# Third stage of a fused attention and two-layer feed-forward kernel as seven block products for eight, slopes through DRAM, outputs summed in PSUM

## The chip, the cores and the metric

One NeuronCore of a Trainium2 chip runs the whole program. The metric is the device time of one execution in microseconds (us); a kernel is judged by the median of several runs. Engines are named as the profile names them: PE (matmuls) and PEld (its weight loads), DVE (vector engine), ACT (scalar engine), POOL and SP, which here mostly issue DMAs.

## The reference

Inputs are float64 in DRAM. Attention is over 4 batches, 12 heads, 448 positions and 64 columns; after it come two feed-forward layers over 1792 tokens.

```python
scores = scale * np.matmul(q, k.transpose(0, 1, 3, 2)) - np.log(S)
attn = 1.0 / (1.0 + np.exp(-scores))
x = np.matmul(attn, v)            # as 1792 x 768
h = np.maximum(np.maximum(x @ w1, x @ w2), x @ w3)      # 768 wide
y = h @ w_out                                            # 768 wide
a = y @ w_in                                             # 2048 wide
g = np.maximum(a, 0.0) + alpha * np.minimum(a, 0.0)      # "slopes"
out = g @ w_out2                                         # 768 wide
```

## The kernel before

Every operand of a matmul is kept as a high and a low part (two tiles of float32r, the low one the remainder), and a product of two operands is three matmuls: low by high, high by low, high by high. Weights come as pairs of 32-bit words in halves of 128 x 384 (`load_half`); `word_ops` (L180) makes float32 of a half with two ACT and three DVE operations (one of them a shift), and `split_ops` (L210) writes the two parts with a cast on ACT and a subtraction on DVE.

Activations are held transposed: 128 features on the partitions, tokens in the columns. The stages after attention are these.

- *First feed-forward product* (x by w1, w2, w3), in `ff1` (L614): 9 units of two feature blocks each, with the tokens in two halves `g`. One unit multiplies a 2 x 2 grid of blocks in seven products for eight (the Winograd form of Strassen's scheme): `unit_ops` (L243) forms seven factors from four weight halves, `form_ops` (L284) seven factors from four blocks of x, and `product` (L644) runs product `k` of unit `u` for half `g`: 9 matmuls of 448 columns into one of three banks X, V, W. At `k` = 0 ACT copies X into V, at 3 and 4 it copies X to the side; these copies stand between two products on the same bank. `evict` takes each finished block from PSUM and keeps the largest of three.
- *Second stage*, the c groups (`c_group`, L699): 24 groups of 18 matmuls of 448 columns. h is partly stored to and reloaded from DRAM through POOL's queue (`hd`, `reload`). y goes straight into the high and low tiles `yt`.
- *Third and fourth stage*, `ff2` (L781): 8 rounds `s` of two feature blocks of 128. `d_group` (L836) multiplies y by w_in, plainly: 18 matmuls for a block of 128 features by 512 tokens; the last 256 tokens are taken as one mixed group. `prelu` (L797) makes the slopes: two Relus on ACT, a join and a split. `e_tile` (L859) multiplies the round's two slope blocks by w_out2 for three tiles of 512 tokens: 6 matmuls into a bank, which DVE adds to an accumulator in SBUF (`acc`). `e_short` (L887) does the last 256 tokens with the slopes as the stationary operand, 384 columns. In the last round the sums are transposed and stored by `store` (L930).

The program is written out in one order by a planner of its own. Work for ACT and DVE is put on lists (`op`, L133), and `advance(cols)` (L138), called after each group of matmuls, takes from them what is ready, as far as a credit in columns goes; an operation costs its columns plus 150, and `STEP` is 1700. DVE's credit is at most what one call gives, ACT's two thirds of it. `need` and `need_ops` force what the next matmul wants. Each engine then runs its instructions in that order, waiting on semaphores.

SBUF slots come from pools of fixed size (`room`, L67; `wslot`, 23 weight slots, L72); a pool that is closed gives its room to the next.

Of the kernel before, what the change touches and what calls it, by code (L numbers as in the profile page):

```python
# [16 lines left out]
P = 128  # L17
# [4 lines left out]
def kernel(  # L22
# [44 lines left out]
    room = {"a": 28, "b": 48, "c": 24, "y": 4}  # L67
# [4 lines left out]
    def wslot(nm, dt=F32):  # L72
        return wpool.tile([P, HF], dt, tag="ws", name=nm, bufs=23)
# [10 lines left out]
    SK = 2  # L84
# [5 lines left out]
    for m in range(KDM):  # L90
        halves += [(w_o1, "col", m, h) for h in range(2)]
    for s in range(KF2 // SK):
        for w, kind in ((w_in, "col"), (w_o2, "row")):
            for f in range(SK):
                halves += [(w, kind, SK * s + f, h) for h in range(2)]
# [29 lines left out]
    class Op:  # L125
        def __init__(self, engine, cols, fn, deps, gate):
            self.engine, self.cols, self.fn, self.deps, self.gate = engine, cols + 150, fn, deps, gate
            self.step = None

# [3 lines left out]
    def op(engine, cols, fn, *deps, gate=None, soon=False):  # L133
        o = Op(engine, cols, fn, [d for d in deps if d is not None], gate)
        (urgent if soon else flow).append(o)
        return o

    def advance(cols, free=False):  # L138
# [3 lines left out]
        for todo in (urgent, flow):  # L142
            n = 0
            while n < len(todo):
                o = todo[n]
                if (
                    (free or o.engine == "Q" or credit[o.engine] > 0)
                    and all(d.step is not None and d.step < now[0] for d in o.deps)
                    and (o.gate is None or o.gate())
                ):  # L150
                    o.fn()
                    o.step = now[0]
                    if o.engine != "Q":
                        credit[o.engine] -= o.cols
# [6 lines left out]

    def need_ops(*ops):
        while any(o.step is None for o in ops):
            assert now[0] < 99999
            advance(0, free=True)

    def need(*dsts):
        for _ in range(99):
            if all(len(d) == 2 for d in dsts):
                return  # L170
            advance(0, free=True)
        raise AssertionError("an operand that nothing makes")
# [7 lines left out]
    def word_ops(z):  # L180
# [26 lines left out]
        o = op("A", 2 * HF, first, gate=lambda: z in since and now[0] > since[z] + 2)  # L207
        return op("D", 3 * HF, whole, o)

    def split_ops(dst, nm, src, pool, w, *deps, seen=lambda x: x, put=lambda x: x, **kw):  # L210

        def hi():
            dst[0] = wslot(f"{nm}h", F32R) if pool == "w" else slot(f"{nm}h", pool, w, F32R)
            nc.scalar.copy(put(dst[0]), seen(src()))  # L214

        def lo():
            dst[1] = wslot(f"{nm}l", F32R) if pool == "w" else slot(f"{nm}l", pool, w, F32R)
            nc.vector.tensor_sub(put(dst[1]), seen(src()), put(dst[0]).bitcast(F32))

        return op("D", w, lo, op("A", w, hi, *deps, **kw), soon=kw.get("soon", False))  # L220

    def conv_ops(z, gate=None):
        if z >= NZ:
            return
        wsp[z] = {}
        o = word_ops(z)
        if halves[z][1] == "col":
            split_ops(wsp[z], f"w{z}", lambda: word[z], "w", HF, o, gate=gate)
        else:
            split_ops(  # L230
                wsp[z], f"w{z}", lambda: word[z], "w", HF, o, gate=gate,
                seen=lambda x: x.rearrange("p (g m j) -> p m g j", g=4, m=HK),
                put=lambda x: x.rearrange("p (m g j) -> p m g j", g=4, m=HK),
            )

# [7 lines left out]
    def unit_ops(u):  # L243

        z = 4 * u
        f = wf[u] = [{} for _ in range(7)]
        t = {}

# [13 lines left out]
        def cut(k, src, *deps):  # L262
            gate = (lambda: (u - 1, k, 1) in made) if u else None
            return split_ops(f[k], f"f{u}_{k}", src, "w", HF, *deps, gate=gate)
# [5 lines left out]
        w2, w3 = word_ops(z + 2), word_ops(z + 3)  # L270
# [8 lines left out]

    wf = {}  # L280
    xf = {(g, c, r): {} for g in range(2) for c in range(7) for r in range(HK)}
    x32, fdone = {}, {}

    def form_ops(i):  # L284

        g, r, n = i // 12, i % 12 // 4, i % 4
        B11, B21, B12, B22 = (4 * (i // 4) + z for z in range(4))
        T1 = ("T", B12)

        def cut(c, src, *deps):  # L290
            pool = "b" if g == 0 or (r == 0 and c in (0, 1, 2)) else "a" if r < HK - 1 else "c"
            fdone[B11, c] = split_ops(
                xf[g, c, r], f"x{g}_{c}_{r}", lambda: x32[src], pool, TW, *deps,
                gate=lambda: pool in pools,
            )

        def t1():
            x32[T1] = slot(f"t1_{i}")
# [11 lines left out]
        if n == 0:  # L310
            cut(0, B11)
        elif n == 1:
            cut(1, B21)
        elif n == 2:
            fdone[B11, "t1"] = op("D", TW, t1)
            cut(2, T1, fdone[B11, "t1"])
        else:
            o3 = op("D", TW, t3, fdone[B11, "t1"])
            o2 = op("D", TW, t2, fdone[B11, 2])
            cut(3, T1, o2)  # L320
            cut(4, B12, o3)
            cut(5, B21, op("D", TW, t4, o2, fdone[B11, 1]))
            cut(6, B22)

    def attention(apool, ps_s, ps_v):
# [180 lines left out]
        def to_x(i):  # L506
            x32[i] = slot(f"x{i}")
            nc.scalar.copy(x32[i], pv.pop(i)[:, :S])
            form_ops(i)
# [28 lines left out]
        for i in range(0, n, 2):  # L538
            for z in range(2):
# [7 lines left out]
                if i + z == 18:  # L547
                    unit_ops(0)
# [33 lines left out]
    yt, ht, hd = {}, {}, {}  # L582
# [31 lines left out]
    def ff1(ps_m, dpool, swap):  # L614
        NU = 3 * HK
        cur, banks, side = {}, {}, {}

        def evict(u, g, i, t, src, other=None):

            j = u % 3  # L620
# [14 lines left out]
            if j == 2:  # L635
# [4 lines left out]
                else:  # L640
                    ht[m, t] = {}
                    split_ops(ht[m, t], f"h{m}_{t}", lambda: c, "b", TW, soon=True)

        def product(u, k, g):  # L644
            left = wf[u][k]
            need(left, *(xf[g, k, r] for r in range(HK)))
# [4 lines left out]
                        tuple(xf[g, k, r][x] for x in range(2)),  # L651
# [5 lines left out]
            nm = f"b{u}_{g}"  # L657
# [27 lines left out]
        def reload(m, t, gate, later):  # L685
            ht[m, t] = {}
            pool = "b" if t < 2 else "y"
            s = {}

            def load():  # L690
# [344 lines left out]
```

## Time and profile before

| | us |
|---|---|
| median of 3 runs | 929.83 (927.98 to 934.37) |
| profiled execution, its own time | 934.59 |
| its span, first to last instruction | 932.8 |
| PE busy | 922.8 |
| DVE busy | 613.3 |
| ACT busy | 446.4 |
| POOL busy | 71.7 |

All numbers from a trace are of the one profiled execution. A span is shorter than that execution's time by what lies before its first and after its last instruction. Matmuls overlap, so a matmul's own duration is longer than its share of a stretch: prices are read as a stretch divided by its count. A row of a stretch gives the stretch, its length, the busy times of PE, PEld, DVE, ACT and POOL with their counts, PEclk (the granted share of PE's full clock), the DMA engines' busy share and GB/s.

### The profile page before, as it was taken

The numbers are of one execution on the slowest core, as the hardware profiler recorded it, in microseconds if no ns is written. First come the engines' busy times: TensorE is split into PE (matmuls) and PEld (weight loads), VectorE is DVE, ScalarE is ACT, GpSimd is POOL, SyncE is SP. The second block draws the span as 40 slices with busy tenths as digits, with TensorE's granted clock in tenths as the row PEclk, the third lists the DMA queues.
The fourth block names the chain that finished last, engine by engine and source line by source line (L and its number), as shares of the span: only waits on it lengthen the run. The fifth ranks groups of instructions, "written<-read, shape, count | busy, mean of one in ns | idle before, by whom it ended". The sixth has DMA issues, their size and how long they took to land.

```text
span 932.8 us, 12606 instructions
## 1 busy us (share of the span) xinstructions
PE 922.8 (99%) x4712; PEld 758.7 (81%) x4712; DVE 613.3 (66%) x1187; ACT 446.4 (48%) x878; POOL 71.7 (8%) x115
## 2 busy tenths in 40 slices
PE   9999999999999999999999999999999999999997
PEld 5555548999999999989988888888888888888886
DVE  5888886677566568653454367676666866568675
ACT  5888886434433445442366551634506345063410
POOL 4433310001001001100000000000000000000001
PEclk9999999999999999999999999999999999999999
DMA  7888451333113224311221211212112121122126
GB/s 156 149 174 145 98 114 37 100 87 114 49 45 135 68 68 148 113 44 58 68 70 51 63 39 52 67 51 68 35 51 69 51 68 34 51 69 52 33 66 172
DMA packets 148573, 74.24 MB, mean 80 GB/s; under 512 B 94128, under 2 KB 144656, under 8 KB 148512
## 3 DMA queue, kind: packets, MB, share of 16 engines
q1 hardware_dynamic: 140704, 57.60, 24.5%
q0 software_dynamic: 5664, 14.98, 4.8%
q10 hardware_dynamic: 2144, 0.85, 0.3%
q8 instruction: 37, 0.61, 0.3%
q14 instruction: 24, 0.20, 0.1%
HBM read 64.23 MB, written 9.18 MB: 79 GB/s over the span
## 4 chain that ended last, share of the span: by engine, by line
PE 96%; ACT 2%; DMA 1%; DVE 1%; issue 0%; SPq 0%; ACTq 0%; DVEq 0%
PE d L604 25%; PE e L604 21%; PE c L604 9%; PE b_0X L604 7%; PE b_1X L604 7%; PE pav L485 6%; PE sc L464 6%; PE b_1W L604 4%; PE b_0W L604 4%; PE e_short L906 4%; PE b_1V L604 2%; PE b_0V L604 2%; ACT a L475 1%; DMA kr<-in_k_dram 0%; DMA kn<-in_k_dram 0%; DVE accs L917 0%
## 5 line engine op out<-in xcount | busy, mean ns | idle before, releaser
L820 DVE SCALAR_TENSOR_TENSOR r<-n,nalpha,r 128x512 f32<-128x512 f32 (+1 forms) x64 | 43.1, 683 | 100.5 <-ACT n L817 99.4
L879 DVE TENSOR_TENSOR acc<-e,acc 128x512 f32<-128x512 f32 x126 | 86.7, 688 | 23.9 <-PE e L604 21.7
L816 ACT ACTIVATE r<-d 128x512 f32<-128x512 f32 (+1 forms) x50 | 29.5, 590 | 146.9 <-PE d L604 146.9
L475 ACT ACTIVATE a<-sc,bias_s 128x896 f32<-128x896 f32 x84 | 82.1, 1014 | 13.4 <-PE sc L464 13.2
L485 PE MATMUL pav<-a,vt 128*64 128x448 f32 (+1 forms) x384 | 70.3, 551 | 0.0
L188 ACT ACTIVATE wt<-wr 128x384 f32<-128x384 f32 x112 | 61.8, 551 | 11.5 <-DMA wr<-in_moe_w_dram 5.9
L203 DVE CUSTOM_DVE_ANT_0 wt<-wr,wt 128x768 uint16<-128x768 uint16 x112 | 62.5, 558 | 3.9
L195 DVE SCALAR_TENSOR_TENSOR wr<-wr 128x384 uint32<-128x384 uint32 x112 | 62.1, 554 | 1.1
L191 ACT ACTIVATE wr<-wr 128x384 uint32<-128x384 uint32 x112 | 61.9, 553 | 0.0
L485 PEld LDWEIGHTS pav<-a,vt 128*64 128x64 f32 (+1 forms) x384 | 21.0, 135 | 38.5 <-issue 36.5
L194 DVE TENSOR_SCALAR wt<-wt 128x384 uint32<-128x384 uint32 x112 | 39.8, 355 | 14.2 <-ACT wt L188 14.2
L934 POOL DMA_DIRECT2D out_dram<-o x6 | 3.9, 663 | 525.4 <-DVE o L854 525.4
L725 DVE TENSOR_TENSOR yl<-c,yh 128x448 fp32r<-128x448 f32 (+5 forms) x36 | 14.2, 421 | 41.6 <-ACT yh L721 29.9
L386 POOL DMA_DIRECT2D vt<-in_v_dram x46 | 35.4, 771 | 63.9 <-PE pav L485 63.9
L464 PE MATMUL sc<-qh,kh 64*128 64x448 f32 x192 | 38.2, 394 | 2.1 <-ACT f_2h L214 1.3
L721 ACT CAST yh<-c 128x448 fp32r<-128x448 f32 (+5 forms) x36 | 12.2, 375 | 50.2 <-PE c L604 50.2
L464 PE MATMUL sc<-ql,kh 64*128 64x448 f32 x192 | 35.4, 365 | 0.0
L464 PE MATMUL sc<-qh,kl 64*128 64x448 f32 x192 | 35.1, 361 | 0.0
L464 PEld LDWEIGHTS sc<-qh,kh 64*128 64x128 f32 x192 | 18.0, 184 | 20.6 <-ACT a L475 6.1
L817 ACT ACTIVATE n<-d 128x512 f32<-128x512 f32 (+1 forms) x50 | 29.2, 585 | 0.0
L673 ACT COPY u<-b_0X 128x448 f32<-128x448 f32 x18 | 9.6, 533 | 39.7 <-PE b_0X L604 39.7
L239 DVE TENSOR_TENSOR u<-b_0W,u 128x448 f32<-128x448 f32 x12 | 7.5, 624 | 31.5 <-ACT u L673 26.3
(1834 smaller groups left out, 2668.5 us busy)
## 6 DMA issues: line engine op xcount, KB each, us to landing
wr<-in_moe_w_out_dram SPq DMA_DIRECT2D x44, 384.0 KB, 3.6
wr<-in_moe_w_dram SPq DMA_DIRECT2D x36, 384.0 KB, 3.6
wr<-in_moe_w_in_dram SPq DMA_DIRECT2D x32, 384.0 KB, 3.6
kr<-in_k_dram SPq DMA_DIRECT2D x92, 56.0 KB, 2.9
qr<-in_q_dram SPq DMA_DIRECT2D x92, 56.0 KB, 2.6
vt<-in_v_dram POOLq DMA_DIRECT2D x46, 96.0 KB, 3.2
hd<-mx POOLq DMA_DIRECT2D x16, 224.0 KB, 2.2
hr<-hd POOLq DMA_DIRECT2D x16, 224.0 KB, 3.7
```

Of the source, the lines that this page charges most:

```text
L188: nc.scalar.activation(st["T"].bitcast(F32), st["r"][:, :, 1].bitcast(F32), AF.Abs, scale=2.0**-112)
L191: nc.scalar.activation(st["r"][:, :, 0], st["r"][:, :, 0], AF.Copy, scale=2.0**-29)
L194: nc.vector.tensor_scalar(st["T"], st["T"], 3, None, ALU.logical_shift_left)
L195: nc.vector.scalar_tensor_tensor(out=st["r"][:, :, 0], in0=st["r"][:, :, 1], scalar=0x80000000, in1=st["r"][:, :, 0], op0=ALU.bitwise_and, ...
L203: nc.vector.tensor_tensor(out=st["T"], in0=st["r"][:, :, 0], in1=st["T"], op=ALU.add)
L464: nc.tensor.matmul(sc[:, j, :S], kx[r, c0 : c0 + P], qx[r], start=(start and z == 0), stop=(stop and z == 2),)
L475: nc.scalar.activation(a, sc[:, :, :S], AF.Sigmoid, bias=bias_s, scale=scale)
L485: nc.tensor.matmul(pv[i][j * D : (j + 1) * D, :S], vts[i][r, j, c, :], a[r, j, :], start=start, stop=stop,)
L604: nc.tensor.matmul(ps[:, : rh.shape[-1]], lt, rh, start=(start and z == 0), stop=(stop and z == len(mms) - 1), skip_group_check=True,)
L820: nc.vector.scalar_tensor_tensor(out=r_, in0=n_, scalar=nalpha[:, m : m + 1], in1=r_, op0=ALU.mult, op1=ALU.add,)
L879: nc.vector.tensor_tensor(out=acc[m, t], in0=ps, in1=acc[m, t], op=ALU.add)
L906: nc.tensor.matmul(ps, lt, rh, start=(f == 0 and i == 0), stop=(f == SK - 1 and i == 2))
```

## The change

The third stage is done like the first. y blocks are first copied to float32, then `form_ops` makes seven factors of each four blocks (`yf`); `unit_ops` makes those of w_in; 8 further units `u` = 9 to 16 run through `product`. `evict` hands their blocks to a new `prelu`, which stores the slopes as float32 to DRAM (`gd`). The c groups go in another order (four blocks that belong together follow each other), some of the conversions into other pools. Two larger pools, "a" and "c", give way to "e" and "l" at the end of the stage.

The fourth stage (`ff3`) then runs by token tiles: 48 steps, one for a tile `t` of 512 tokens and a block `f` of slopes, each 6 x 3 matmuls. Six banks, one for each output block, are summed over six blocks `f` and later over ten for the first two tiles, over all sixteen for the third. Slopes are reloaded through POOL's queue into three raw buffers and split again. All of w_out2 is kept in SBUF; it is converted 8 halves before the stage and 24 in it. The last 256 tokens come at the end, 48 matmuls into one bank for each of four blocks. `need_ops` now forces only what its operations depend on; before, it took everything that was ready.

```diff
-    room = {"a": 28, "b": 48, "c": 24, "y": 4}
+    room = {"a": 76, "c": 24, "e": 16, "l": 32}
...
+    blocks = [m for r in range(HK) for m in (r, r + HK)]
...
     def need_ops(*ops):
+        chain = [o for o in ops if o.step is None]
+        for o in chain:
+            chain += [d for d in o.deps if d.step is None and d not in chain]
         while any(o.step is None for o in ops):
...
-            advance(0, free=True)
+                for o in [o for o in todo if o in chain]:
+                    if ready(o) and (
+                        o.gate is None or o.gate()
+                    ):
+                        emit(o)
+                        todo.remove(o)
+            if len(urgent) + len(flow) == n:
+                advance(0, free=True)
...
+        def prelu(u, g, i, t, src, add=None):
+            f, b = 2 * (u - ND0) + i, 2 * g + t
+            s, o = {}, None
+            if add is not None:
+                o = op("D", TW, lambda: tensor_op(add, src, add, ALU.add), soon=True)
+            def parts():
+                x = src if add is None else add
+                s["r"], s["n"] = slot(f"r{f}_{b}"), slot(f"n{f}_{b}")
+                nc.scalar.activation(s["r"], x, AF.Relu)
+                nc.scalar.activation(s["n"], x, AF.Relu, scale=-1.0)
+            def join():
+                nc.vector.scalar_tensor_tensor(
+                    out=s["r"], in0=s["n"], scalar=nalpha[:, f : f + 1], in1=s["r"],
+                    op0=ALU.mult, op1=ALU.add,
+                )
+            def store():
+                if f not in gd:
+                    gd[f] = dpool.tile([P, B * S], F32, tag=f"g{f}", name=f"gd{f}")
+                nc.gpsimd.dma_start(out=gd[f][:, b * S : (b + 1) * S], in_=s["r"])
+            o = op("A", 2 * TW, parts, o, soon=True)
+            stored.append(op("Q", 0, store, op("D", TW, join, o, soon=True)))
...
         def evict(u, g, i, t, src, other=None):
+            if u >= ND0:
+                return prelu(u, g, i, t, src, other)
...
+        def y_home(g, c, r):
+            return "c" if g and (r == HK - 1 or (r == 1 and c >= 3)) else "a"
+        def y_gate(g, r):
+            if g == 0:
+                return lambda pool: r < HK - 1 or ("c", KDM - 1, 1) in made
+            if r == 0:
+                return lambda pool: ("c", KDM - 1, 1) in made
+            return lambda pool: ("c", *((HK, 3) if pool == "a" else (KDM - 1, 3))) in made
...
-            for t, (c0, w) in enumerate(spans):
-                c, e = max(c0, b * S), min(c0 + w, b * S + S)
-                if c < e:
-                    y_ops(t, m, slice(c - c0, e - c0), ps[:, c - b * S : e - b * S], e - c)
+            def out():
+                x32["y", m, b] = slot(f"y{m}_{b}", "c")
+                nc.scalar.copy(x32["y", m, b], ps[:, :TW])
+            o = op("A", TW, out, soon=True)
+            blk = [("y", r + HK * n, 2 * g + c) for c in range(2) for n in range(2)]
+            form_ops(f"y{g}{r}", 2 * t + i, blk, (g, r), yf, y_home, y_gate(g, r), o)
...
+        units(ND0, ND1 - 1, begin, (
+            (0, 1), (0, 0), (1, 1), (2, 1), (1, 0), (3, 1), (2, 0), (4, 1), (3, 0), (5, 1), (4, 0),
+            (6, 1),
+        ), lambda x: x == (5, 1) and started.append(ff3(ps_m, turn_left, E0)))
+        run = started[0]
+        swap()
+        for k in range(5, 7):
+            step(ND1 - 1, k, 0)
+        need_last = list(stored)
+        run(need_last)
...
+    def ff3(ps_m, turn_left, E0):
+        F1 = 6
+        passes = [(t, *x) for x in ((0, F1), (F1, KF2)) for t in range(2)] + [(2, 0, KF2)]
+        steps = [(t, f, f == f0, f == f1 - 1) for t, f0, f1 in passes for f in range(f0, f1)]
...
+        for n, (t, f, _, _) in enumerate(steps):
+            s, load = load_g(t, f, functools.partial(raw_g, n, t, f))
+            o = op("Q", 0, load, gops[n - 3] if n > 2 else None, gate=lambda n=n: n < 2 or "e" in pools, lag=4 if n > 2 else 1)
+            gops.append(
+                cut_g(
+                    s,
+                    lambda x, t=t, f=f: pools["e"].tile(
+                        [P, EW], F32R, tag=f"g{x}", name=f"g{x}{t}_{f}", bufs=3
+                    ),
+                    lambda s=s: s["t"],
+                    EW,
+                    o,
+                    lambda n=n: "e" in pools and (n < 3 or ("e", n - 3) in made),
+                    True,
+                )
+            )
+        for n in range(2 * E0, 2 * KF2):
+            pool = "e" if n < 4 * E0 else "l"
+            conv_ops(NE + n, pool, gate=lambda pool=pool: pool in pools)
...
+        def run(stored):
+            ps, done = {}, []
+            for n, (t, f, start, stop) in enumerate(steps):
+                if n == 2:
+                    need_ops(*stored)
+                    turn_left()
+                z = NE + 2 * f
+                need(wsp[z], wsp[z + 1])
+                need_ops(gops[n])
+                for m in range(KDM):
+                    if start:
+                        ps[m] = bank(ps_m, f"e{t}_{f}_{m}")
+                    a, b = three(weight(z, m), tuple(gt[t, f][x] for x in range(2)))
+                    group(ps[m], a + b, start=start, stop=stop)
+                    if stop:
+                        leave(t, m, ps[m], f < F1 or t == 2, f == KF2 - 1, done)
+                    if m == KDM - 1:
+                        made.add(("e", n))
+                    advance(2 * STEP // 5)
...
+            for n in range(HW // P):
+                for h in range(2):
+                    p = bank(ps_m, f"es_{n}{h}")[:, :HF]
+                    for f in range(KF2):
+                        need_ops(gops[len(steps) + f])
...
+                        advance(STEP // 3)
+                    x = pools["l"].tile([P, HF], F32, tag="acc", name=f"os{n}{h}", bufs=2 * KDM)
+                    nc.scalar.copy(x, p)
```

`leave` copies a finished bank to an accumulator with ACT, or adds it with DVE in a tile's second pass, and then has DVE transpose it; a tile's four stores go out on SP's queue.

## Rows read from the trace of the kernel before

**Rows 1.** The page's first lines: the span, and busy us, share and count of PE.

```profile
span 932.8 us, 12606 instructions
PE 922.8 (99%) x4712; PEld 758.7 (81%) x4712; DVE 613.3 (66%) x1187; ACT 446.4 (48%) x878; POOL 71.7 (8%) x115
```

**Rows 2.** Waits of PE from 142 us on: in total us, times, longest.

```profile
PE e_short L906 <- ACT g L826: 1.1, 1, 1.1
PE c L604 <- DVE h_3l L218: 0.2, 1, 0.2
```

**Rows 3.** The chain in order of time: start us, us, what, instructions.

```profile
174.44 1.86 PE b_1V L604 x9
...
380.90 14.89 PE c L604 x72
...
465.91 28.74 PE d L604 x132
494.64 24.49 PE e L604 x108
519.13 4.31 PE e_short L906 x24
...
868.52 24.48 PE d L604 x108
...
917.48 4.32 PE d L604 x36
923.46 2.80 PE e_short L906 x14
926.28 2.17 DVE accs L917 x4
```

**Rows 4.** Engines by stretch (us): first stage's products, c stage; us, busy us, PEclk.

```profile
142.60:375.30 232.70, 232.70 (x1128) 211.30 (x1127) 155.04 (x307) 105.37 (x224) 13.02 (x24) 1.00 0.27 85
375.30:466.00 90.70, 90.45 (x444) 82.81 (x443) 46.24 (x106) 34.43 (x88) 4.27 (x8) 1.00 0.24 71
```

**Rows 5.** Groups of ACT, 142.6 to 375.3 us: count, busy us, mean ns, idle.

```profile
L188 ACT ACTIVATE wt<-wr 128x384 f32<-128x384 f32 x36 | 19.8, 550 | 5.9 <-DMA wr<-in_moe_w_dram 5.9
L673 ACT COPY u<-b_0X 128x448 f32<-128x448 f32 x18 | 9.6, 533 | 39.7 <-PE b_0X L604 39.7
L214 ACT CAST f_2h<-wu 128x384 fp32r<-128x384 f32 x8 | 4.1, 517 | 0.0
```

**Rows 6.** Groups of ACT, 466 to 581 us.

```profile
L816 ACT ACTIVATE r<-d 128x512 f32<-128x512 f32 x12 | 7.2, 599 | 19.0 <-PE d L604 19.0
L826 ACT CAST g_2h<-r 128x512 fp32r<-128x512 f32 x4 | 2.5, 622 | 1.6 <-DVE r L820 1.6
L913 ACT COPY accs<-e_short 128x384 f32<-128x384 f32 x4 | 1.9, 480 | 2.3 <-PE e_short L906 2.3
```

**Rows 7.** Groups of DVE, 142.6 to 375.3 us.

```profile
L203 DVE CUSTOM_DVE_ANT_0 wt<-wr,wt 128x768 uint16<-128x768 uint16 x36 | 20.1, 558 | 1.2
L194 DVE TENSOR_SCALAR wt<-wt 128x384 uint32<-128x384 uint32 x36 | 12.8, 355 | 9.2 <-ACT wt L188 9.2
L239 DVE TENSOR_TENSOR u<-b_0W,u 128x448 f32<-128x448 f32 x12 | 7.5, 624 | 31.5 <-ACT u L673 26.3 <-PE b_0W L604 5.2
L218 DVE TENSOR_TENSOR f_1l<-wt,f_1h 128x384 fp32r<-128x384 f32 x8 | 4.4, 554 | 1.6 <-ACT f_1h L214 1.6
```

**Rows 8.** Groups of DVE, 466 to 581 us.

```profile
L820 DVE SCALAR_TENSOR_TENSOR r<-n,nalpha,r 128x512 f32<-128x512 f32 x12 | 9.0, 751 | 30.8 <-ACT n L817 30.5
L829 DVE TENSOR_TENSOR g_2l<-r,g_2h 128x512 fp32r<-128x512 f32 x4 | 2.8, 689 | 1.4 <-ACT g_2h L826 1.4
```

**Rows 9.** DMA issues: queue, count, KB each, median us to landing.

```profile
wr<-in_moe_w_out_dram SPq DMA_DIRECT2D x44, 384.0 KB, 3.6
...
hd<-mx POOLq DMA_DIRECT2D x16, 224.0 KB, 2.2
hr<-hd POOLq DMA_DIRECT2D x16, 224.0 KB, 3.7
```

More of the change, by code (lines that the diff above doesn't have):

```diff
@@ L89 @@
     NB = len(halves)
-    for m in range(KDM):
+    blocks = [m for r in range(HK) for m in (r, r + HK)]
+    for m in blocks:
         halves += [(w_o1, "col", m, h) for h in range(2)]
[L92 to L95, printed above, removed]
+    ND = len(halves)
+    for fp in range(KF2 // 2):
+        halves += [(w_in, "col", 2 * fp + z // 2, z % 2) for z in range(4)]
+    NE = len(halves)
+    for f in range(KF2):
+        halves += [(w_o2, "row", f, h) for h in range(2)]
     NZ = len(halves)
@@ L147, in advance @@
                     (free or o.engine == "Q" or credit[o.engine] > 0)
-                    and all(d.step is not None and d.step < now[0] for d in o.deps)
+                    and ready(o)
                     and (o.gate is None or o.gate())
                 ):
[L151 to L154, printed above, removed]
+                    emit(o)
                     todo.pop(n)
@@ L741, in ff1, with units @@
-        order = [(0, k, 0) for k in (0, 2, 1, 3)]
-        order += [(0, 0, 1), (0, 4, 0), (0, 2, 1), (0, 5, 0), (0, 1, 1), (0, 6, 0), (0, 3, 1)]
-        order += [(1, 0, 0), (0, 4, 1), (1, 1, 0), (0, 5, 1), (1, 0, 1), (0, 6, 1), (1, 1, 1)]
-        order += [(u, k, g) for u in range(1, L) for k in range(7) for g in range(2) if (u, k) > (1, 1)]
-        order += [(L, k, g) for k, g in (
+        def units(first, last, begin, end, before=None):
+            u, v = first, first + 1
+            o = [(u, k, 0) for k in (0, 2, 1, 3)]
+            o += [(u, 0, 1), (u, 4, 0), (u, 2, 1), (u, 5, 0), (u, 1, 1), (u, 6, 0), (u, 3, 1)]
+            o += [(v, 0, 0), (u, 4, 1), (v, 1, 0), (u, 5, 1), (v, 0, 1), (u, 6, 1), (v, 1, 1)]
+            o += [(n, k, g) for n in range(v, last) for k in range(7) for g in range(2) if (n, k) > (v, 1)]
+            o += [(last, k, g) for k, g in end]
+            for x in o:
+                if before and x[0] == last:
+                    before(x[1:])
+                step(*x)
@@ new lines, in leave, with room @@
+        def leave(t, m, ps, first, final, done):
+            def room():
+                if t not in ot:
+                    ot[t] = pools["l"].tile(
+                        [P, EW // 32, KDM, 32], F32, tag="ot", name=f"ot{t}", bufs=2
+                    )
+                turn(t, m)
+            if first:
+                acc[t, m] = pools["l"].tile([P, EW], F32, tag="acc", name=f"acc{t}_{m}", bufs=2 * KDM)
+                nc.scalar.copy(acc[t, m], ps)
+                spend("A", EW)
+            else:
+                tensor_op(acc[t, m], ps, acc[t, m], ALU.add)
+                spend("D", EW)
+            if final:
+                done.append(op("D", EW, room))
+                if m == KDM - 1:
+                    op("Q", 0, lambda: put(t), *done)
```

552 lines of the change are left out of this document (252 added, 300 removed).

## The prediction

> **What bounds the kernel now.** I read the page's busy shares first. TensorE (PE) is busy 922.8 us of a span of 932.8 [rows 1], so what the change does to PE's own instructions counts in full, and another engine counts only where PE comes to wait for it. The waits of PE come next: from 142 us to the end they add up to 1.3 us, in two waits [rows 2]. There are no stalls to win; a gain has to come from fewer or shorter matmuls, and a loss from new waits. The chain of work in order of time then gives the price of each kind of matmul, as stretch by count: a block product of the first feed-forward stage is 9 matmuls of 448 columns in 1.86 us, 206.7 ns each; the c groups run at the same pace (72 in 14.89 us); e (512 columns) takes 24.49 us for 108, 226.8 ns each; e_short (384 columns) 4.31 us for 24, 179.6 ns each; d, which mixes 512 and 256 columns, 28.7 us for 132 [rows 3]. An e group puts six matmuls into a bank, a d group eighteen, and both take 24.5 us for 108 matmuls of 512 columns, so leaving a bank for the next costs nothing. The granted clock is 1.00, the 2.4 GHz level, throughout [rows 4].
>
> The last look is at the two engines that feed PE, by stage. In the block products of the first stage VectorE (DVE) is busy 155 of 232.7 us and ScalarE (ACT) 105; in the c stage 46 and 34 of 90.7 [rows 4]. This is the room that the change will use up.
>
> **What is removed from PE.** The d stage is, in the chain, seven rounds of 28.7 us, then 24.48 and 4.32 us: 229.8 us [rows 3]. In its place stand 8 units of 7 products for 2 halves of the tokens, 9 matmuls each: 8 x 14 x 9 = 1008 matmuls of 448 columns. The same form runs before in the first stage, so its price is a row, not a guess: 1008 x 206.7 ns = 208.3 us. The saving is 21.5 us, less than an eighth (28.7), because the products also go from 512 columns to 448 and a narrower matmul costs more for each column: 226.8 ns for 512, 206.7 for 448.
>
> The Trainium skill, page "TensorE: Matmul & The Clock Gate", section "Back-to-back issue gap", gives the gap of a single warm matmul as columns / 2.4 plus 2.5 ns, so 189.2 ns for 448. The rows do not agree: 206.7 for 448 columns. By the page the old stage would cost 217.7 us and the new one 190.7, a saving of 27.0 us for 21.5.
>
> The e stage keeps 3 tiles x 16 x 6 x 3 = 864 matmuls of 512 columns, and the short block 2 x 2 x 16 x 3 = 192 of 384: 864 x 226.8 ns = 195.9 us and 192 x 179.6 ns = 34.5 us. Summed into fewer, longer accumulations they cost PE the same. From the first d to the last e_short before is 465.91 to 926.26, 460.35 us, with the one wait of 1.1 us in it [rows 2, 3]; after it is 208.3 + 195.9 + 34.5 = 438.7 us. That is 21.6 us less. The c stage keeps its 24 groups of 18 matmuls in another order, at no price.
>
> **The tail.** After the last matmul four additions by DVE (2.17 us) stand on the chain, and then the store [rows 3]. After the change the last short block is copied once by ACT from PSUM, 0.48 us by the same shape's copy [rows 6], then stored. That saves 1.7 us. The transposes and stores of the third tile lie under the 34.5 us of short blocks, and each tile has two more DMAs on SP's queue (its four stores no longer alternate with POOL), with nothing behind them there but two stores of short blocks. Removed without effect: the additions of every round (126 on DVE), which nothing waited for.
>
> So far 21.6 + 1.7 = 23.3 us.
>
> **What is added, and what hides it.** All prices of ACT and DVE below are from [rows 5 to 8]. *c stage.* Each output block is copied by ACT (0.53), and six sets of four blocks are combined (24 DVE operations of 0.62) and cut into high and low parts (42 casts of about 0.57 between the 384 and the 512 forms, 42 subtractions of 0.62): 36.6 us on ACT and 41 on DVE. With the weights (8 halves at 1.6 and 2.0 us), the cuts of h (8 pairs) and the first unit's factors the stage asks for some 62 us of ACT and 74 of DVE in 91 us of PE: it fits. Eleven cuts of the last two blocks wait for the last c group, since their slots hold h until then. They take about 6.3 us of ACT; the first product that needs one of them comes after four other products, 7.4 us, and the next ones at intervals of about two products. The blocks are also done in that order, so I cost this at nothing; with the cover gone it would be 6 us.
>
> *d stage.* For one unit, 26.0 us of PE: ACT has 4 weight halves (two operations of 0.55 each), 7 casts (0.52), 6 PSUM copies (0.53) and 16 Relu parts (0.55, between the 448 copy and the 512 Relu): 20.0 us, 77%. DVE has 4 x (0.56 + 0.56 + 0.35), 4 sums and 7 subtractions of 0.55, 4 additions of 0.62 and 8 joins of about 0.68 (0.75 for 512): 19.9 us, 76%. In the last unit 8 halves of w_out stand for the factors: 25 of 26 us on ACT and 24 on DVE. That is the tightest stretch ahead of the end, but w_out is needed a pair of halves for every step of 4.1 us later, not at once. The 64 stores of slopes go through POOL's queue, which holds nothing else then; stores of this size land in 2.2 us [rows 9].
>
> *The trip through DRAM.* Each of 48 steps of e loads 512 columns, in three raw buffers. A buffer's round is landing 3.7 us [rows 9], cast 0.62, subtraction 0.69: 5.0 us in three steps, 12.2 us. The first steps read slopes of the first unit, written 180 us earlier. So it is hidden with 7 us to spare. The Trainium skill, page "SBUF — State Buffer", section "Who interferes with whom", speaks against this move: descriptors of DMAs that GpSimd issues are held up while VectorE runs an operation in a two-port mode. The shift on the weights, 0.35 us and one for each half [rows 7], would be such an operation, and even one in front of every load would leave the 7 us nearly whole. The trace before has stores and reloads of h in that queue, landing in 2.2 and 3.7 us while DVE was two thirds busy, and shows no hold-up of its own.
>
> *Opening of e.* Here 24 halves of w_out are still to be converted. The kernel's planner gives DVE 680 columns for each 0.68 us group; a half costs 1836 of them and a slope tile 662, so 1.86 halves a step are put in. In time that is 1.86 x 2.02 + 0.69 = 4.45 us of DVE in a step of 4.08 us. DVE falls 0.37 us a step behind, for 13 steps: 4.8 us. Slope tiles are written out about 11 groups, 7.5 us, ahead of their use; 4.8 + 0.69 fits into that with 2 us left. The weights' landing of 3.6 us [rows 9] with three buffers (3.6 + 1.1 + 1.5 = 6.2 us for three halves, wanted every 6.6) is as close. If one of these covers is gone, what is late is the next slope tile, and PE with it.
>
> **Sum.** For handovers (c to d, d to e, e to the short blocks) and the opening of e I add a loss. The lower bound is 0, as in every handover of before; the upper is 9 us, all of DVE's 4.8 us twice over, once for itself and once for the loads. The chain of Relus, join and cut ahead of the last short block takes 1.66 us, from the end of the last d (917.48 + 4.32) to 923.46 [rows 3]. Three places with such a chain half covered make 2.5 us; I take this, near to the lower end, since the rows show hardly a wait. The profiled execution took 934.59 us, of which 932.8 are its span; it becomes 934.59 - 23.3 + 2.5 = 913.8 us. It lay 4.8 us above the median of the three runs, 929.83. Against the median: 929.83 - 20.8 = **909.0 us**.
>
> **Rivals.** *A: the opening of e is not covered.* DVE at over 100% of PE's pace and ACT near it speak for it; the lead of 7.5 us against. Loss 6 to 13 us: 913 to 920 us. *B: the copies between products are late (the other side).* In every unit 6 times, 48 times in all, PE waits for an ACT copy of a bank (the start of V, the two side sums) that must be done within one product, 1.86 us. The copy takes 0.53, so 1.3 us are left. With a pair of Relus (1.1) and a pair of weight operations (1.1) put ahead of it that only then begin, it comes 2.2 + 0.53 - 1.86 = 0.87 us late; 48 x 0.87 = 42 us, and the time is 948 us. It decides from 0.49 us a copy, where the gain is gone. Against it: in the first stage the same copies, with ACT at 45%, cost PE nothing [rows 2, 4], and the planner limits what stands ahead of a copy. With a third of that lateness (14 us) the time is 921. *C: the slopes land late*, held up in POOL's queue while DVE is near full. A buffer's round would have to grow from 5 to over 12 us; the landings of before speak against it. At 13 us a round it is 0.27 us a step, 13 us in all: 920 us. *D: a narrower matmul costs no more for a column*: the stage falls by a full eighth, 28.7 us for 21.5, and the time is 902 us; against it stand the 206.7 ns of the products before [rows 3]. The Trainium skill's page on TensorE, section named above, would give 903.5. That the change leaves PE's work as it was can't be: the count of matmuls is in the loops.
>
> **Chances.** Forecast (0 to 6 us lost, 906 to 913) 0.62; A 0.17; B 0.11, in which 0.05 at over 939; C 0.06; D 0.04. About 1% is what a measurement of this kernel can tell from no change, so faster is below 920.5. The forecast, D, A but for 0.02 and half of C go there: 0.84; the rest of A and C and 0.06 of B stay within 1%: 0.11; slower 0.05. The range goes from the sum without a loss less the 1.9 us by which the lowest run lies under the median, 904, to the upper end of A, 919.
>
> **What would show it.** In the profile after: a unit of d in 26.0 us at 9 matmuls in 1.86; steps of e at 4.08 us; PE's waits under 5 us in all; DVE near full in the first 55 us of e; one copy between the last matmul and the store. A PE wait on ACT's copies inside d would be B; on slope tiles early in e, A; on the cast behind a DMA, C. A c or e matmul slower than before would make the whole sum wrong.

## The result, and the profile after

| | before | after |
|---|---|---|
| median, us | 930.24 (927.98 to 934.37) | 902.67 (902.51 to 905.14) |
| ratio, with its 95% interval | | 0.9705 (0.9667 to 0.9743) |
| profiled execution, its own time | 934.59 | 902.51 |
| its span | 932.8 | 900.7 |

The change saves 27.6 us. The forecast was 20.8, and its range ended at 904, 1.3 us above the time. The sign, the place of the gain and waits of PE under 5 us came out as forecast; the price of a matmul did not.

The first lines of the page after, to be held against [rows 1]: PE stays at 99% of a span that is shorter.

```profile
span 900.7 us, 12994 instructions
PE 891.9 (99%) x4652; PEld 755.8 (84%) x4652; DVE 584.2 (65%) x1145; ACT 493.2 (55%) x962; POOL 137.8 (15%) x239
```

The waits of PE after, from 142 us to the end (in total us, times, longest). [Rows 2] had two, of 1.3 us; the 1.1 us ahead of e_short are gone and nothing has come instead.

```profile
PE c L645 <- DVE h_3l L246: 0.2, 1, 0.2
```

The chain of work after, in order of time (start us, us, what, instructions). A product of the third stage is 9 matmuls in 1.82 us, where the product of the first stage took 1.86 before [rows 3]. The fourth stage is 864 matmuls in 196.04 us (226.9 ns) and 192 in 34.56 us (180.0 ns), as before. One copy stands between the last matmul and the store.

```profile
503.40 1.82 PE u_1X L645 x9
...
508.87 1.83 PE u_0W L645 x9
...
665.74 196.04 PE e L645 x864
861.78 34.56 PE es L1045 x192
...
896.36 0.48 ACT os L1051
```

Windows after: first stage, third stage, opening of e (four stretches, of which the first and the last), columns as in [rows 4]. The first stage took 232.70 us before [rows 4] and takes 228.35, although its matmuls are the same. In the third stage ACT is busy 144 of 202 us (71%) and DVE 151 (74%). The third stage's row begins with its second product. In the opening of e DVE is at 14.3 and 14.6 of 16.3 us, 87 and 90%.

```profile
143.11:371.46 228.35, 228.35 (x1126) 211.39 (x1127) 151.63 (x300) 102.84 (x219) 17.27 (x32) 1.00 0.30 92
463.27:665.74 202.47, 202.47 (x1001) 187.45 (x999) 150.56 (x296) 144.26 (x312) 35.58 (x66) 1.00 0.41 139
665.70:682.00 16.30, 16.30 (x73) 13.38 (x72) 14.26 (x31) 11.04 (x24) 4.67 (x9) 1.00 0.83 250
714.70:731.00 16.30, 16.30 (x73) 13.49 (x73) 14.62 (x32) 13.52 (x29) 2.15 (x4) 1.00 0.71 209
```

### The profile page after: what moved, and what is told of

It reads as the page before. It is cut to its first block, busy times and chain, and to the rows that moved or that the text cites. A ratio compares the mean times of both kernels' runs of the same rounds, so it can differ in the third digit from the quotient of the medians.

```text
span 900.7 us, 12994 instructions
## 1 busy us (share of the span) xinstructions
PE 891.9 (99%) x4652; PEld 755.8 (84%) x4652; DVE 584.2 (65%) x1145; ACT 493.2 (55%) x962; POOL 137.8 (15%) x239
## 4 chain that ended last, share of the span: by engine, by line
PE 96%; DVE 1%; ACT 1%; DMA 1%; issue 0%; SPq 0%; DVEq 0%
PE e L645 22%; PE u_0X L645 14%; PE u_1X L645 14%; PE c L645 10%; PE u_0W L645 7%; PE u_1W L645 7%; PE pav L522 6%; PE sc L501 6%; PE es L1045 4%; PE u_0V L645 3%; PE u_1V L645 3%; DMA kr<-in_k_dram 0%; ACT a L512 0%; DMA kn<-in_k_dram 0%; DVE kt L459 0%
## 5 line engine op out<-in xcount | busy, mean ns | idle before, releaser
L512 ACT ACTIVATE a<-sc,bias_s 128x896 f32<-128x896 f32 x84 | 82.2, 1016 | 13.5 <-PE sc L501 13.3
L930 ACT CAST gh<-gr 128x512 fp32r<-128x512 f32 (+1 forms) x48 | 29.8, 621 | 91.8 <-PE e L645 83.8
L935 DVE TENSOR_TENSOR gl<-gr,gh 128x512 fp32r<-128x512 f32 (+1 forms) x48 | 32.9, 684 | 72.5 <-ACT gh L930 72.5
L682 POOL DMA_DIRECT2D gd<-r x64 | 34.8, 544 | 263.4 <-DVE r L674 240.4
L268 DVE TENSOR_TENSOR u<-u_0W,u 128x448 f32<-128x448 f32 x28 | 17.5, 624 | 53.5 <-ACT u L748 48.6
L748 ACT COPY u<-u_0X 128x448 f32<-128x448 f32 x34 | 18.1, 534 | 55.7 <-PE u_0X L645 55.5
L674 DVE SCALAR_TENSOR_TENSOR r<-n,nalpha,r 128x448 f32<-128x448 f32 x64 | 42.1, 680 | 7.0 <-ACT n L671 7.0
L907 POOL DMA_DIRECT2D gr<-gd x48 | 25.9, 539 | 134.3 <-DVE gl L935 121.4
L737 ACT COPY u_0V<-u_0X 128x448 f32<-128x448 f32 x17 | 8.8, 518 | 50.5 <-PE u_0X L645 50.5
L748 ACT COPY u<-u_1X 128x448 f32<-128x448 f32 x34 | 18.1, 533 | 32.3 <-PE u_1X L645 32.3
```

Source lines behind the costliest of these rows:

```text
L512: nc.scalar.activation(a, sc[:, :, :S], AF.Sigmoid, bias=bias_s, scale=scale)
L674: nc.vector.scalar_tensor_tensor(out=s["r"], in0=s["n"], scalar=nalpha[:, f : f + 1], in1=s["r"], op0=ALU.mult, op1=ALU.add,)
L748: nc.scalar.copy(side[g, k], banks[X][:, :TW])
```

## The experiments

**The same two kernels again.** The unchanged first stage had become 4.3 us shorter. Either the pace of a matmul differs from one execution to the next, or the change had altered something ahead of the third stage. Both kernels ran again as they are, the one after a third time later.

> The kernel before, unchanged, profiled once more. The profiled execution shown ahead of the prediction ran every 448-column matmul of the first feed-forward stage at 206.7 ns, the changed kernel's at 202.6. Theory 1, the pace is fallen into anew in each execution: this profile may show either pace, and executions spread from 928 us (all at 202.6) to 934 (206.7 through the first stage, 1134 matmuls x 4.1 ns = 4.6 us more). Theory 2, the pace belongs to the kernel, for instance to where its tiles lie in SBUF: 206.7 ns again in the whole stage, spans near 932.8 us in the profile.

> The changed kernel, unchanged, profiled once more. Theory 1 (the pace of 448-column matmuls is fallen into anew in each execution): executions spread upward from 902.5 us, up to 913 where all 2574 of them run at 206.7 ns for 202.6. Theory 2 (it belongs to the kernel): 902.5 to 903 us each time and 202.6 ns throughout.

Before: 929.20 us (927.96 to 933.37, 10 runs). After: 902.17 us (900.82 to 902.44, 4 runs). The profiled execution of before had a span of 926.6 us this time. Its chain:

```profile
145.21 1.83 PE b_0V L604 x9
...
459.79 28.73 PE d L604 x132
...
917.33 2.79 PE e_short L906 x14
920.14 2.17 DVE accs L917 x4
```

The same line that took 1.86 us in [rows 3] takes 1.83 here, and d is at 28.73 as it was. So the 448-column matmul has two paces, and an execution of the same program shows one or the other: 206.7 ns from start to start, evenly, or 202.6 ns in the mean, in a pattern (203, 202, 203, 199, 207 ns, over and over). Matmuls of 512 and 384 columns cost the same in both executions, but none of them ran while the slower pace lasted. The granted clock is 1.00, the 2.4 GHz level, in both, so it isn't the clock. The trace of before that the forecast was made from holds both. In its timeline (start us, us, engine, line, operation) the even pace lasts to one break in the c stage:

```profile
396.65 0.37 PE L604 MATMUL c<-h_3l,w36h 128*128 128x448 f32 x1
397.09 0.47 PE L604 MATMUL c<-h_3h,w37l 128*128 128x448 f32 x1
397.74 0.47 PE L604 MATMUL c<-h_3l,w37h 128*128 128x448 f32 x1 [0.18 <-DVE h_3l L218]
```

From 397.74 on, after steps of 0.44 and 0.65 us between starts where 0.2 is usual (a record seems to be missing in the first), that trace runs at 202.6 ns too. The repeat of after shows the quicker pace throughout; no execution of after came near the 913 us that the slower one would take all the way.

**The eighth product put back.** Theory: the gain is the count of PE's matmuls alone. Rival: a part of it comes from the other moves (outputs summed in PSUM, fewer DVE additions). The product is computed into a bank that nothing reads: 16 times 9 matmuls.

```diff
+                if u >= ND0:
+                    group(bank(ps_m, nm + "Y"), mms)
```

> The changed kernel with the matmul saving of the third stage taken back and nothing else: at the end of each unit's set of seven products, for each half of the tokens, nine more matmuls of 448 columns repeat the last product into a bank that nothing reads; 144 in all. Theory 1, the whole gain of that stage is PE's count of matmuls: 144 x 202.6 ns = 29.2 us more, 931.9 us, no gain left but the tail and the lack of a full eighth in the price of narrower matmuls. Theory 2, part of the gain is from elsewhere (order, fewer forced operations, fewer additions): still faster than before by 5 us or more, under 925 us. Theory 3, the longer stage gives ACT and DVE room that they lacked: under 931 by some us.

930.45 us (929.09 to 934.35, 10 runs), ratio to before 1.0013 (0.9997 to 1.0029). With the eighth product, all the rest of the change together is worth nothing that can be measured: the 28 us are the product's. The rest is itself a sum. Eight products in 448 columns take 233.5 us, 3.7 more than the old stage's 229.8; 1.7 come back between the stage and PE's last matmul, and 0.5 behind it. From the first matmul of the third stage to PE's last one the trace takes 464.04 us for 435.04 without: 29.0 us for 144 matmuls, 201.4 ns each, near 202.6. Its third stage in the windows, again all of it PE:

```profile
460.10:693.50 233.40, 233.40 (x1153) 216.29 (x1152) 153.76 (x301) 147.78 (x318) 36.82 (x69) 1.00 0.37 124
```

**The DRAM trip of the slopes: one raw buffer, then two.** The prediction had 5.0 us of a round against 12.2 us in three buffers. With one buffer a round no longer fits into a step of 4.08 us; with two it has 8.2.

```diff
-            ... tag="graw", name=nm, bufs=3),)
+            ... tag="graw", name=nm, bufs=1),)
-            o = op("Q", 0, load, gops[n - 3] if n > 2 else None, ...
+            o = op("Q", 0, load, gops[n - 1] if n > 2 else None, ...
```

> The changed kernel with one raw buffer for reloaded slopes instead of three, each load put in only after the step before it has been split. It sizes the cover of the trip through DRAM. Theory 1, a buffer's round is issue 0.54, landing 3.2, cast 0.62, subtraction 0.69 = 5.05 us, now once in every step of 4.08 us: PE waits 0.97 us in most of the 48 steps, some 40 to 47 us more, 943 to 950 us, the waits on the subtraction. Theory 2, the loads hide under what was split ahead all the same: within 3 us of 902.7. Theory 3, the queue is slower than its rows say: over 960 us.

One buffer: 944.64 us (943.48 to 949.42), 42 us more. PE's waits, in total us, times, longest:

```profile
PE e L645 <- ACT gh L930: 14.8, 12, 3.0
PE e L645 <- DVE gl L935: 8.7, 32, 1.4
```

The rows of waits add up to 23.5 us, and the fourth stage is 43 us longer. Two stretches of e in the windows, and the longest wait in the timeline:

```profile
690.00:720.00 30.00, 25.71 (x98) 19.09 (x99) 22.80 (x49) 21.88 (x46) 3.26 (x6) 0.94 0.67 188
750.00:780.00 30.00, 27.42 (x113) 20.51 (x112) 11.42 (x18) 3.73 (x6) 3.22 (x6) 1.00 0.26 72
```

```profile
785.01 0.51 PE L645 MATMUL e<-gh,w96l 128*128 128x512 f32 x1 [2.96 <-ACT gh L930]
785.74 0.50 PE L645 MATMUL e<-gl,w96h 128*128 128x512 f32 x1 [0.22 <-DVE gl L935]
...
787.30 0.63 PE L645 MATMUL e<-gh,w96h 128*128 128x512 f32 x1
787.73 0.63 PE L645 MATMUL e<-gh,w96l 128*128 128x512 f32 x1
```

At 226.8 ns a stretch of 30 us holds 132 matmuls; 98 and 113 are in it, the 113 at the full granted clock. The starts of the 864 matmuls of e tell where the 42 us went. 23.7 are the idle times themselves. The clock falls to the 1.2 GHz level only at the three waits of 2.5 to 3.0 us, and the matmuls behind them start mostly 427 ns apart (787.30 and 787.73): 4.8 us in all. At the other waits, of at most 1.4 us, it stays at 1.00. The remaining 13.5 us lie right behind a wait, long or short: the first start after it comes some 0.2 us later than the idle time tells, and the next one about 0.1. The expectation had the sum right (40 to 47 us) but put it down to 0.97 us of wait on the subtraction in most steps; the waits on it are 0.3 us each, and the longest ones are on the cast.

> The changed kernel with two raw buffers for reloaded slopes instead of three. With one buffer a step took 4.5 us in the trace where PE has 4.08. Theory 1, that is a buffer's round, and with two it has 8.2 us: hidden, within 1 us of 902.2 us, no wait of PE in e. Theory 2, the third buffer is needed while the weights' loads share the DMA engines in the first 57 us of e (busy share 0.75): 2 to 6 us more, all of it there.

Two buffers (`bufs=2`, `gops[n - 2]`): 901.72 us (900.76 to 905.46), no wait of PE in e. The trip is hidden with two buffers; the third covers nothing that can be measured. The round of 5.0 us was about the right size (with one buffer a step takes 4.7 us in the median and 5.0 in the mean): one buffer is too few, two are enough.

**The lead of the slope tiles in the opening of e.** The prediction let DVE fall 4.8 us behind under a lead of 7.5. Here the low part of each reloaded slope tile is computed three times: 1.38 us more DVE in each step.

```diff
-                    nc.vector.tensor_sub(dst[1][:, c], x, dst[0][:, c].bitcast(F32))
+                    for _ in range(3 if soon else 1):
+                        nc.vector.tensor_sub(dst[1][:, c], x, dst[0][:, c].bitcast(F32))
```

> The changed kernel with the subtraction that writes each low slope tile of the 48 steps done three times, 1.38 us more of DVE in every step, unknown to the planner. It sizes the cover in the opening of e. Measured without it: DVE is busy 48.5 of the first 57.1 us of e and PE waits for nothing. Theory 1, the slope tiles' lead of 7.5 us is what covers a late DVE: 14 steps x 1.38 = 19.3 us on top of 48.5 make 67.8, 10.8 us behind PE, of which 7.5 are covered: 3 to 5 us of waits early in e, 905 to 908 us, nothing later. Theory 2, there is no lead to speak of: 9 to 13 us, 911 to 916. Theory 3, the room is larger than both: within 1 us of 902.2.

916.78 us (916.43 to 920.73), 14.6 more than after. The waits of PE and the windows of the opening:

```profile
PE e L645 <- DVE gl L936: 6.1, 5, 1.7
PE e L645 <- ACT acc L1003: 3.6, 2, 2.8
PE e L645 <- DVE w90l L246: 1.3, 1, 1.3
```

```profile
665.70:682.00 16.30, 16.21 (x71) 13.25 (x71) 15.85 (x32) 7.68 (x17) 2.71 (x5) 1.00 0.57 174
682.00:698.40 16.40, 13.66 (x56) 10.19 (x56) 15.99 (x33) 11.93 (x25) 2.17 (x4) 1.00 0.66 190
...
714.70:731.00 16.30, 12.21 (x46) 9.05 (x45) 15.31 (x29) 11.53 (x25) 1.61 (x3) 0.90 0.60 171
```

DVE is full from the first stretch, and in the second PE already stands 2.7 us of 16.4; a first wait of 1.7 us, up to 665.79, lies nearly all ahead of the first row. The theory that the lead absorbs most of it is wrong; the one without a lead to speak of is nearest. The rows of waits add up to 11.0 us, and without any lead DVE would fall 10.7 us behind by the expectation's numbers (67.8 us of work in 57.1). The waits are not on slope tiles alone: weights and the copies of finished banks are late as well. In the last row, at the wait of 2.8 us, the clock falls to 0.90. What protects this stretch is that DVE has some 14% free over the four stretches; of the 7.5 us of lead nothing shows.

**The copies between products, twice.** Rival B needed 0.49 us of lateness a copy. Each of the 48 copies of the third stage is made twice, 0.53 us more in each place.

```diff
-                nc.scalar.copy(banks[V][:, :TW], banks[X][:, :TW])
+                for _ in range(2 if u >= ND0 else 1):
+                    nc.scalar.copy(banks[V][:, :TW], banks[X][:, :TW])
...
-                nc.scalar.copy(side[g, k], banks[X][:, :TW])
+                for _ in range(2 if u >= ND0 else 1):
+                    nc.scalar.copy(side[g, k], banks[X][:, :TW])
```

> The changed kernel with the ACT copies that stand between two products on one bank done twice in the third stage: 48 copies, 0.53 us more each, ACT at some 85% of that stage for 71%. It sizes the cover of rival B. Theory 1, the copies have 1.86 us and with 1.07 for both 0.8 are left; what stands ahead of them on ACT is done earlier: no wait of PE, within 1 us of 902.2. Theory 2, a pair of Relus or of weight operations often stands just ahead: waits of 0.2 to 0.9 us in some of the 48, 905 to 930 us. Where there are waits, the pace after them may change too.

901.63 us (900.99 to 904.84). The only waits of PE are two of 0.2 us, and the third stage's window shows ACT at 81%:

```profile
461.00:666.00 205.00, 205.00 (x1012) 189.58 (x1012) 147.98 (x292) 166.58 (x356) 35.28 (x65) 1.00 0.40 136
```

B is out with more than half a microsecond a copy to spare. This profiled execution is the longest of its runs, 904.84, and happens to show both paces of one form of matmul in one chain, of the first stage and of the third:

```profile
304.44 1.86 PE u_0W L645 x9
...
503.49 1.82 PE u_0X L645 x9
```

**What ends the slower pace.** Theory: any break in the row of equal matmuls. A matmul of 64 columns stands ahead of each first product (34 places).

```diff
+                lt, rh = mms[0]
+                nc.tensor.matmul(bank(ps_m, nm + "Z")[:, :64], lt, rh[:, :64], start=True, stop=True)
```

> The changed kernel with one extra matmul of 64 columns, into a bank of its own that nothing reads, ahead of the first product of each unit and half of the tokens: 34 of them, some 0.05 to 0.1 us each, 2 to 4 us in all. It asks whether a break in the row of 448-column matmuls lets the pace be chosen anew. Theory 1, any break does: stretches between two breaks (14 products) show 202.6 or 206.7 ns by chance, and the time is up to 8 us more than the breaks alone. Theory 2, only a wait of PE does, or the pace is set once: 202.6 ns in every stretch (or 206.7 in every one), 904 to 906 us.

905.80 us (905.10 to 906.00, 4 runs). The short matmuls also disturb later sums, by a way that no run here shows; only the times are read here. The chain around the second of the short matmuls:

```profile
146.58 1.86 PE u_0V L645 x9
148.44 1.86 PE u_0X L645 x9
150.30 0.03 PE u_1Z L735
150.33 1.90 PE u_1X L645 x9
152.22 1.82 PE u_0X L645 x9
```

This execution began at 206.7 ns; the short matmul at 150.30 ended that, and the 32 behind it left the quicker pace as it was. Against the 901.7 us of the two kernels just above, on the same chip, the 34 cost 4.1 us, 0.12 us each. To use it cheaply, three matmuls of the first unit are split in 64 and 384 columns, in both kernels (in the kernel before under the same lines of its `product`):

```diff
+            if z == 4 and broken[0]:
+                broken[0] = 0
+                for c in (slice(0, 64), slice(64, TW)):
+                    nc.tensor.matmul(ps[:, c], lt, rh[:, c], start=False, stop=False, skip_group_check=True)
+                continue
...
+            if u == 0 and g == 0 and k in (2, 1, 3):
+                broken[0] = 1
```

> The changed kernel with three breaks early in the first stage: in the second, third and fourth product of the first unit one of the nine matmuls is split into 64 and 384 columns of the same bank. Same sums. Theory 1, a break ends the slow pace (206.7 ns for 448 columns) and the quick one (202.6) stays: no execution over 903.5 us, median 901 to 902.5 with at most 0.4 us for the breaks; the first stage at 202.6 ns in the profile whatever it began with. Theory 2, the spread between executions is not from the pace: some of them over 904 us, as without breaks (904.84 and 905.14 of 20 so far).

> The kernel before with the same three breaks. Theory 1 (a break ends the slow pace): no execution over 930.5 us, where without breaks 7 of 19 lay over 930.8, up to 933.5; median 928.3 to 929. Theory 2: a third of them over 930.8 us as before, median 929.5.

> The changed kernel unchanged, for its spread beside the one with breaks. Theory 1: median within 0.5 us of the kernel with breaks, but some executions 4 to 5 us higher (904 to 906). Theory 2: the same spread as with breaks.

After with breaks: 901.18 us (900.60 to 902.77, 5 runs), against 901.31 (900.95 to 901.55, 4 runs) for after as it is, on the same chip. Neither set has an execution over 903 us, so by their times the two theories can't be told apart. In the timeline with breaks, the starts lie 0.21 us apart up to the first split and mostly 0.20 from it on:

```profile
144.00 0.37 PE L652 MATMUL u_0W<-x_2l,f_2h 128*128 128x448 f32 x1
144.21 0.44 PE L650 MATMUL u_0W<-x_2h,f_2h 128*128 128x64 f32 x2
144.49 0.37 PE L652 MATMUL u_0W<-x_2h,f_2h 128*128 128x448 f32 x1
144.69 0.36 PE L652 MATMUL u_0W<-x_2h,f_2l 128*128 128x448 f32 x1
144.89 0.37 PE L652 MATMUL u_0W<-x_2l,f_2h 128*128 128x448 f32 x1
```

Before with breaks: 929.57 us (928.29 to 931.82, 12 runs), ratio to before 1.0003 (0.9993 to 1.0014). The theory wanted no run over 930.5, and five of twelve are over 930.8, where two of 17 without breaks on this chip are. So breaks end the even pace where it is there, but that pace explains at most the longest runs of before; the smaller spread has another source. One is seen: attention, whose matmuls no run here changes, ended between 140.5 and 143.0 us in the profiles. No gain is to be had from the breaks.

## Why the prediction was right or wrong

Like is compared with like by the first repeated profile of before (span 926.6, quicker pace throughout) and the one after (900.7).

| part, us | before again | after | difference |
|---|---|---|---|
| up to the first stage | 141.3 | 143.0 | +1.7 |
| first stage and c stage | 228.2 + 90.2 | 228.3 + 90.0 | -0.1 |
| third stage's start to PE's last matmul | 462.1 | 435.0 | -27.1 |
| from there to the end | 4.9 | 4.4 | -0.5 |

The first line is attention's own spread; without it the sum is -27.7, and the medians differ by 27.6.

*The price of the products: the step that failed.* "The same form runs before in the first stage, so its price is a row, not a guess": the row was one execution's. It held 206.7 ns; the stage ran at 202.6: 1008 x 4.1 ns = 4.1 us. Third stage: 229.8 before, 112 products of 1.8236 = 204.2 us after, 25.6 saved for 21.5 forecast. A second stretch of the same trace, the c stage behind 397.74 us, had the right price for the same 448 columns; the prediction read one c row of 14.89 us from ahead of the break [rows 3] and took it as a confirmation. The prediction also set the profiled execution's 4.8 us over the median aside as a difference to be scaled away. Its first stage took 4.4 us more than in the repeat; the span is 6.2 us longer in all.

*Rival D*, 902 us, has the nearest time but not its mechanism. A narrower matmul still costs more for a column: 202.6 / 448 = 0.452 ns against 226.8 / 512 = 0.443. The stage gave 25.6 us, not an eighth. The Trainium skill, "TensorE: Matmul & The Clock Gate", section "Back-to-back issue gap", gives an estimate of 189.2 ns by its formula for a single matmul. Neither pace agrees, and the measured numbers decide.

*The fourth stage* was right: 195.9 and 34.5 us forecast, 196.04 and 34.56 measured. The longer accumulations in PSUM cost PE nothing that shows.

*The tail* was right in its sum by luck and wrong in its parts. The prediction took the end of PE's last row in the chain [rows 3], 926.26, for the end of its work. But the chain leaves PE there for the additions, and PE goes on beside them. The last matmuls in the timeline, in the trace of the forecast and in the repeat:

```profile
927.34 0.52 PE L906 MATMUL e_short<-w111h,g 128*128 128x384 f32 x2
```

```profile
921.20 0.52 PE L906 MATMUL e_short<-w111h,g 128*128 128x384 f32 x2
```

So PE's stretch from the first d was 1.6 us longer than the 460.35 us of the forecast, and the tail shorter by as much. In the repeat PE ends at 921.7, and the four additions run from 920.14 to 922.31: they stand out by 0.6 us, the copy after by 0.5, so their going is worth 0.1 us, not 1.7. The other 0.4 us of the table's last line lie between them and the end of the last store. What is left of the 27.1 us after the third stage's 25.6 is 1.5, which holds PE's wait ahead of the last short block. Together that is 2.0 us outside the third stage, where the forecast's terms come to 1.8 (23.3 less 21.5).

*The loss of 2.5 us for handovers and the opening of e* did not come: one wait of 0.2 us. In the opening of e the working gave DVE 109% of PE's time, with 1.86 weight halves a step. The trace shows 25 halves over 16 steps, 1.56 a step, and DVE at 86% over the four stretches. That the planner's cap on DVE's credit and the three raw weight buffers hold the halves back is read from the code and was not tried alone. Rival A was thus wrong by its premise, but nearer than the forecast made it: 1.38 us a step more, and it costs 14.6 us.

*The covers* that were claimed held. c to d: no wait of PE there. Third stage: ACT 77% and DVE 76% forecast, 71 and 74% measured; rival B needed late copies, and even doubled ones are not late. DRAM trip: hidden with two buffers of the three. Rival C did not come: the landings after (queue, count, KB each, median us) are, for the stores over the whole execution, for the loads in the opening of e (665 to 731 us) and behind it,

```profile
gd<-r POOLq DMA_DIRECT2D x64, 224.0 KB, 2.4
...
gr<-gd POOLq DMA_DIRECT2D x17, 256.0 KB, 3.9
...
gr<-gd POOLq DMA_DIRECT2D x28, 256.0 KB, 2.9
```

against 2.2 and 3.7 us of the same queue before [rows 9]. The 1.0 us more in the opening points to the DMA engines rather than to DVE: in the run with the low parts computed three times, DVE is fuller there (up to 98%) and the 14 loads land in 3.0 us, with the DMA engines at 0.57 to 0.66 for 0.71 to 0.83. The Trainium skill, "SBUF — State Buffer", section "Who interferes with whom", would have descriptors of this queue held up while DVE runs an operation in a two-port mode. No landing here shows it: none of these medians comes near the 12 us that rival C needs.

The sum, then: 4.1 us for the pace, 2.5 for the loss that did not come and 0.2 for the rest make 6.8, which is 27.6 less 20.8. Against the time itself the forecast is 6.3 us too high, since before had a median 0.4 higher this time. The range failed at its lower end, which went down to a sum without loss but took the price of a matmul as certain. With 4.1 us for the pace it would have begun at 900.

## What to carry to other kernels

Where PE is the bound and never waits, a block product less is worth its matmuls in full, as long as the engines that feed it keep up in every stretch. Here DVE at 90% of one stretch made no wait and at 97% it did. Look at the stretch, not at the mean, and at the free share rather than at a lead, since everything else stands in the same queue. A price per matmul is to be read in several stretches and, where there are any, several executions; if two rows of one shape differ by 2%, the range has to hold both. Work at the very end is worth what sticks out behind the last matmul, not its duration on the chain; the chain's last row of PE need not be PE's last work.

## What the runs showed of the hardware

- The 448-column matmul runs at 206.7 ns (1.86 us for 9) or 202.6 ns (1.82 us for 9), at the same granted clock of 1.00; 512 columns take 226.8 to 226.9 and 384 take 180 ns, each seen only behind the slower pace's end. Each of the 13 profiled executions is in one of the two paces from the start of the first stage. In four it was the slower one, and each time it ended: at gaps of 0.44 and 0.65 us between starts (before), at a 64-column matmul, at a split one, and in the execution with the doubled copies at a start that came only 0.23 us after the last for 0.21. The other direction was seen nowhere. What decides the pace at the start stays open. The timeline of the last of the four:

```profile
371.03 0.37 PE L645 MATMUL u_0W<-x_6h,f_6h 128*128 128x448 f32 x1
371.23 0.39 PE L645 MATMUL u_1X<-x_5h,f_5l 128*128 128x448 f32 x1
371.46 0.36 PE L645 MATMUL u_1X<-x_5l,f_5h 128*128 128x448 f32 x1
371.66 0.36 PE L645 MATMUL u_1X<-x_5h,f_5l 128*128 128x448 f32 x1
```

- Many short waits of PE cost more than their rows tell: 23.5 us of waits made the fourth stage 43 us longer with one raw buffer. Most of the difference is in the starts right behind a wait (13.5 us, 46 waits), less in the clock (4.8 us).
- The granted clock stayed at 1.00 through waits of PE up to 1.7 us and fell to the 1.2 GHz level at each of the four waits of 2.5 to 3.0 us (three with one raw buffer, one with the low parts three times). Behind them 512-column matmuls started 427 ns apart for 227.
